# A row scan, its write to DRAM and its read back, moved ahead of some loads; one filler matmul split in two

## The chip, the cores and the metric

The kernel runs on one core of a Trainium2 chip. The time is device time in microseconds, from the first to the last work of the core. The kernel before takes 364.13 us (median of three runs, 364.1 to 365.35). The engines are TensorE (PE; PEld is its loading of stationary operands), VectorE (DVE), ScalarE (ACT), GpSimd (POOL) and SyncE (SP), which here only issues transfers.

## The reference

Two layers follow each other. The first is a chunked scan over 768 steps for 4 batches of 8 heads, with 32 values and 16 states a head:

```python
log_a = np.log(np.clip(a, 1e-06, 1.0))
cum = np.cumsum(la, axis=-1)                      # within a chunk
y_intra = (C B^T * exp(cum_i - cum_j), causal) x
y_inter = (C state) * exp(cum_i)
state = exp(sum(la)) * state + sum_j B_j x_j exp(cum_end - cum_j)
```

(cut and put in short form). Its output, 3072 tokens by 256, goes through the second:

```python
h = x @ w_in                                       # 256 -> 2048
g = np.maximum(h, 0.0) + alpha * np.minimum(h, 0.0)
return (g @ w_out).astype(np.float32)              # 2048 -> 256
```

In place of exponentials of sums the kernel uses running products of `a`: a product from the start of a chunk up to each step is what `exp(cum)` is.

## The kernel before, in words

**Tiling.** The kernel uses chunks of 128 steps (`Q`), six to a batch, and works on pairs of chunks. Pairs 0 and 1 are treated apart, in `first_two`; pair 2 and the later ones go through the generator `pair`, one stage at a time, between the products of the second layer. The second layer takes groups of 512 tokens (two pairs). Group 0 runs in the loop over `f`, 16 blocks of 128 hidden features: `hidden(0, f)` (L1077) multiplies tokens by `w_in` into a PSUM bank of pool `hp`, which has two banks; ScalarE and VectorE make the activation from it (L1080, L1081) and so free the bank; `output(f - 4)` (L1124) multiplies by `w_out`. Later groups run in `quad` and `product`.

**Order.** All five engines keep the order in which the source issues instructions; nothing is rescheduled. An engine that waits holds all that is behind it. All transfers of this part are issued by SP, one after the other. Transfers reuse eight semaphores in turn, so that each also waits for the one eight places earlier.

**Weights.** `w_in` and `w_out` arrive as 16 pieces of 512 KB each (`load_next`, six buffers), and each is converted to f32 by ScalarE, VectorE and GpSimd (`convert_a`, `convert_b`, `convert`; L270 to L327). Pieces 0, 1, 2, 4, 6 belong to `w_in`, 3, 5, 7 to `w_out`.

**Row products.** For half of the batches, `a` lies as 96 rows of 128 steps. `rows_scan(0)` (L462) makes products from each step to the end of its chunk; `rows_products` (L439) makes those from its start, and writes them to a DRAM scratch named `pf` (L442, 48 KB). `load_products` (L167) reads them back, spread over partitions, into the tile `ap` of a pair (128 KB). Pair 2 uses `ap` in `states` (L637, the step of the state) and in `c_decayed` (L677). `load_spread` (L160) reads clamped rows from another scratch, `z`, into the `abc` tiles of a pair (two transfers of 512 KB); the scans L562 make the decays from them. The hp bank that gram L737 of pair 2 writes is the one that L1081 of block 6 reads.

**Where the moved steps stand.** In `first_two`, after pair 0: two pieces of weights, B, C and x of pair 2 for both its chunks (`load_pair(2, False)`), two more pieces; then pair 1; at the end `rows_scan(0)`, `rows_products()`, `load_spread(2, ...)`. The read back into `ap` of pair 2 stands after `first_two`, behind a piece of weights. `convert_next` issues a further piece where the count of loaded pieces allows it.

**Fillers.** `keep_warm(to, n, cols)` (L335) issues n matmuls of ones on `cols` columns into a PSUM place that is not read, so that TensorE is not idle; each shows as two in the profile.

Of the kernel before, what the change touches and what calls it, by code (L numbers as in the profile page):

```python
# [22 lines left out]
def kernel(  # L23
# [25 lines left out]
    nc = tc.nc  # L49
# [7 lines left out]
    Q = 128  # L57
# [4 lines left out]
    RW = batch // 2 * H * CPB  # L62
# [4 lines left out]
    GT = GC * Q  # L67
# [8 lines left out]
    NB = 2  # L76
# [3 lines left out]
    HALF = NP // 2  # L80
# [16 lines left out]
    gp = ctx.enter_context(tc.tile_pool(name="gp", bufs=16))  # L97
# [6 lines left out]
    def bank(i):  # L104


        return ps_q.tile([P, 512], F32, name="bank", tag=f"q{i}")
# [13 lines left out]
    loads = {}  # L121

    def load_rows(i, eng=nc.sync):

        rows = ld.tile([RW, Q], F32, name="rows")
        eng.dma_start(out=rows, in_=a.rearrange("b h (c t) -> (b h c) t", t=Q)[i * RW : (i + 1) * RW])
        loads["r", i] = rows
# [3 lines left out]
    def load_a(t, b, c, eng=nc.sync):  # L131
        first = a[b, 0:1, c * Q : (c + 2) * Q]
        eng.dma_start(out=t, in_=bass.AP(tensor=first.tensor, offset=first.offset,
                                             ap=[[S, H], [0, N], [1, 2 * Q]]))
# [4 lines left out]
    def load_tokens(dst, src, t0):  # L139


        d = dst.rearrange("p j (h w) -> p j h w", h=H)
        for k in range(2):
            for j in range(2):
                t = t0 + k * Q + j * HQ
                nc.sync.dma_start(out=d[HQ * k : HQ * (k + 1), j],
                                  in_=src[:, t : t + HQ, :].rearrange("h p w -> p h w"))

    def load_spread(gp, b, c):

        for w, t in enumerate(loads["p", gp][1] if gp >= HALF else ()):
            rows = scratch["z", b // 2].rearrange("(b h c) t -> b c h t", b=2, h=H)
            for k in range(2):
                nc.sync.dma_start(
                    out=t[HQ * k : HQ * (k + 1), : 4 * SQ].rearrange("p (h t) -> p h t", h=4),
                    in_=rows[b % 2, c + k, 4 * w : 4 * w + 4].unsqueeze(0)
                    .to_broadcast([HQ, 4, SQ]))
        for k, t in enumerate(loads["p", gp][1] if gp < HALF else ()):
            rows = scratch["z", b // 2].rearrange("(b h c) t -> b c h t", b=2, h=H)[b % 2, c + k]
            nc.sync.dma_start(out=t.rearrange("p (h t) -> p h t", h=H),  # L160
                              in_=rows.unsqueeze(0).to_broadcast([P, H, Q]))

    def load_products(gp, ap):
        b, c = divmod(2 * gp, CPB)
        rows = scratch["pf", b // 2].rearrange("(b h c) t -> b h (c t)", b=2, h=H)
        rows = rows[b % 2, :, c * Q : (c + 2) * Q]
        nc.sync.dma_start(out=ap, in_=rows.unsqueeze(1).to_broadcast([H, N, 2 * Q]))  # L167

    def load_pair(gp, decays=True):


        b, c = divmod(2 * gp, CPB)
        turned = gp > GC
        nat = ldx.tile([P, 3, 2, H * N], F32, name="nat")
        xt = ldx.tile([P, 2, HD], F32, name="xt")

        ap = ldx.tile([P, 2 * Q], F32, name="ap")
        if gp == 0:
            load_a(ap, b, c)
        elif gp > NB:  # L180
            load_products(gp, ap)
        if gp == 0:
            load_rows(0, nc.scalar)
        abc = []
        later = []
        if gp >= HALF:
            load_tokens(nat[:, 0], B[b], c * Q)
        for k in range(2 if gp < HALF else 0):
            ts = slice((c + k) * Q, (c + k + 1) * Q)
            for i, src in enumerate((B,) if turned else (B, C)):  # L190
                eng = nc.scalar if gp == 0 and i else nc.sync
                eng.dma_start(out=nat[:, i, k].rearrange("p (h n) -> p h n", h=H),
                              in_=src[b, :, ts, :].rearrange("h p n -> p h n"))

            def load_x(k=k, ts=ts):
                nc.sync.dma_start(out=xt[:, k].rearrange("p (h d) -> p h d", h=H),
                                  in_=x[b, :, ts, :].rearrange("h p d -> p h d"))

            if gp < NB:
                later.append(load_x)  # L200
            else:
                load_x()
        for load_x in later:
            load_x()
        if gp == 0:
            nc.scalar.dma_start(out=al_n, in_=moe_alpha.rearrange("(k p) -> k p", p=P))
            loads["a", 1] = prep.tile([P, 2 * Q], F32, name="a1")
            load_a(loads["a", 1], b, c + 2)
        for i, src in enumerate((B, C) if turned else ()):


            for e in range(2):
                first = src[b, e : e + 1, c * Q : (c + 2) * Q, :]
                nc.sync.dma_start(out=nat[:, 1 + e, i],
                                  in_=bass.AP(tensor=first.tensor, offset=first.offset,
                                              ap=[[2 * S * N, P // 32], [8 * N, 32], [1, 8 * N]]))
        for k in range(2 if gp >= NB else 0):
            abc.append(lda.tile([P, H * Q], F32, name="abc"))
        loads["p", gp] = nat, abc, xt, ap
        if gp >= HALF:  # L220
            load_tokens(xt, x[b], c * Q)
        if decays:
            load_spread(gp, b, c)

    def load_second():

        rows = scratch["short", 0].rearrange("(b h c) t -> b h (c t)", b=2, h=H)
        nc.sync.dma_start(out=loads["p", 1][3], in_=rows[0, :, 2 * Q : 4 * Q].unsqueeze(1)
                          .to_broadcast([H, N, 2 * Q]))
# [102 lines left out]
    def keep_warm(to, n, cols=2 * Q):  # L332

        for i in range(n):
            nc.tensor.matmul(to[:, :cols], warm.to_broadcast([P, P]), warm.to_broadcast([P, cols]),  # L335
                             start=True, stop=True, skip_group_check=True)
# [29 lines left out]
    zeros = const.tile([P, Q], F32, name="zeros")  # L366
# [38 lines left out]
    held = {}  # L405
# [28 lines left out]
        eng.tensor_scalar(out=out, in0=in_, scalar1=1e-6, scalar2=1.0, op0=ALU.max, op1=ALU.min)  # L434

    def rows_products():
        d0 = held.pop(0)
        rpf = prep.tile([RW, Q], F32, name="rpf")
        nc.vector.tensor_tensor_scan(out=rpf, data0=d0[:, :Q], data1=zeros[:RW], initial=1.0,  # L439
                                     op0=ALU.mult, op1=ALU.add)  # L440
        scratch["pf", 0] = dr.tile([RW, Q], F32, name="pf0")
        nc.sync.dma_start(out=scratch["pf", 0], in_=rpf)  # L442
# [98 lines left out]
    def spare():  # L541

        return ps_h.tile([P, GT], F32, name="hp", tag="hp")
# [272 lines left out]
    def first_two():  # L816
# [90 lines left out]
        def mask(i, cs):  # L907
            n = cs.stop - cs.start
            nc.gpsimd.tensor_tensor(
                out=sm[i][:, cs].rearrange("p k (g m) -> p k g m", g=2),  # L910
                in0=new[i][:, cs].unsqueeze(2).to_broadcast([P, n, 2, 2 * D]),
                in1=hmask.rearrange("p (g m) -> p g m", g=2).unsqueeze(1)
                .to_broadcast([P, n, 2, 2 * D]), op=ALU.mult)
# [35 lines left out]
        def ss():  # L949
            return ps_s.tile([P, 512], F32, name="ss")  # L950
# [8 lines left out]
        def one_at_a_time(i, cs):  # L959
            for c in cs:  # L960
                mask(i, slice(c, c + 1))
# [16 lines left out]
        for r in range(4):  # L978
            scan(0, r, sp[r])
        rows_turn("short", prq)  # L980
        tp, hp = spare(), spare()
        bc0 = turned(nat0, (tp, hp))
        cz0 = spread_c(bc0)
        al_p = ss()
        nc.tensor.transpose(al_p[:, :NF], al_n, ident[:NF, :NF])
        nc.scalar.copy(out=alpha, in_=al_p[:, :NF])
        bn0 = pair_loads(0)
        slopes(alpha)
        keep_warm(hp, 1, GT)
        gram_of(bc0, cz0, sp)  # L990
        dps = dps_in([hp, tp])
        added(dps, bn0, xt0)
# [1 line left out]
                                     data1=starts_a, initial=0.0, op0=ALU.mult, op1=ALU.add)  # L994
# [6 lines left out]
            times(0, r, sp[r])  # L1001
        z1 = first_a(loads["a", 1], nc.vector, lent[1][:, 2:])
        load_next(2)
        load_pair(2, False)
        load_next(2)
        convert_a(*pieces[0], by=nc.vector)
        convert_b(*pieces[0], ways=2)
        y = places([ss(), ss()], [hp, tp])
# [28 lines left out]
        added(dps, bn1, xt1)  # L1037
        states(1, dps, pf1, range(3))
        one_at_a_time(1, range(3))
        keep_warm(second, 1)  # L1040

        def among(i, k):
# [16 lines left out]
        convert_next(first=False)  # L1059
        mask(1, slice(3, 4))  # L1060
        held["pr"] = rows_scan(0)
        rows_products()
        load_spread(2, *divmod(4, CPB))
        prelu_of[2]()
        state[0] = new[1][:, 3]
# [334 lines left out]
    def load_next(n=1):  # L1400
        for p in pieces[loaded[0] : loaded[0] + n]:
            load_weights(*p)
        loaded[0] += n
# [13 lines left out]
    load_next(2)  # L1417
    FIRST = 4
    first_two()
    convert_a(*pieces[3])  # L1420
    convert_b(*pieces[3])
    hidden_two(0, 0, 2 * Q, spare())()
    convert_next(first=False)
    load_products(NB, loads["p", NB][3])
    rest = hidden_two(0, 2, 2 * Q, bank(3))
    rows_turn(0, held["pr"])
    convert_a(*pieces[4])
# [135 lines left out]
```

## Time and profile before

| | us |
|---|---|
| median of 3 runs | 364.13 |
| profiled execution | 364.29 |
| its span | 362.6 |
| TensorE busy | 354.0 |
| VectorE busy | 238.1 |
| GpSimd busy | 203.1 |
| ScalarE busy | 172.1 |

Mean granted clock of TensorE: 0.985. The DMA engines are busy for most of the first 58 us, and lightly after. In the profile "x ← y" at the end of a line names what an engine waited for before it; a time in the first column counts from the start of the span.

### The profile page before, as it was taken

How to read it: one execution, taken by the hardware profiler on the slowest of the kernel's cores; microseconds unless marked ns; L12 is line 12 of the kernel's file. 1: busy time of each engine (PE TensorE's matmuls, PEld its weight loads, DVE VectorE, ACT ScalarE, POOL GpSimd, SP SyncE). 2: the span in 40 equal slices, each digit the busy share in tenths (PEclk: the TensorE clock that was granted, in tenths of full speed). 3: DMA queues.
4: the chain of work that ended last, by engine and by line, in shares of the span. 5: the costliest groups of instructions: out<-in, count | busy, mean ns of one | idle time of the engine just before them, and what ended most of it. 6: DMA issues, size and time to landing. Idle time of an engine off the chain costs nothing.

```text
span 362.6 us, 7773 instructions
## 1 busy us (share of the span) xinstructions
PE 354.0 (98%) x2983; PEld 286.6 (79%) x2983; DVE 238.1 (66%) x483; ACT 172.1 (47%) x391; POOL 203.1 (56%) x227
## 2 busy tenths in 40 slices
PE   7999699999999999999999999999999999999996
PEld 3676366667888888888888888888888888888885
DVE  6787575989846856766656766657866634743363
ACT  3379417634445535635535535535535534453431
POOL 6577347669965947554546545537545546334511
PEclk9999969999999999999999999999999999999999
DMA  7999798504525420510640540530301001001102
GB/s 145 192 206 329 229 233 220 136 2 75 170 63 134 88 54 26 102 50 6 116 86 12 109 86 8 112 87 18 57 2 30 1 2 29 2 1 29 33 0 58
DMA packets 105581, 30.24 MB, mean 83 GB/s; under 512 B 79896, under 2 KB 101448, under 8 KB 105544
## 3 DMA queue, kind: packets, MB, share of 16 engines
q1 hardware_dynamic: 103048, 29.43, 35.5%
q10 hardware_dynamic: 2496, 0.32, 0.6%
q8 instruction: 23, 0.38, 0.4%
q14 instruction: 14, 0.11, 0.1%
HBM read 26.32 MB, written 3.42 MB: 82 GB/s over the span
## 4 chain that ended last, share of the span: by engine, by line
PE 90%; DMA 5%; DVE 3%; ACT 1%; SPq 0%; issue 0%; DVEq 0%
PE bank L1198 33%; PE hp L1223 28%; PE bank L1124 7%; PE ss L1223 6%; PE hp L1077 4%; DMA pf<-rpf 2%; PE ss L782 1%; DMA ap<-pf 1%; PE ss L726 1%; DMA nat<-in_B_dram 1%; PE bank L1191 1%; PE ss L800 1%; PE ss L774 1%; PE hp L737 1%; PE ss L737 1%; DVE dec L562 1%
## 5 line engine op out<-in xcount | busy, mean ns | idle before, releaser
L1280 POOL TENSOR_TENSOR gt<-gt 128x512 f32<-128x512 f32 x58 | 74.1, 1278 | 21.1 <-DVE gt L1208 16.3
L1198 PE MATMUL bank<-gt,w_out 128*128 128x256 f32 x320 | 83.5, 381 | 0.0
L1198 PEld LDWEIGHTS bank<-gt,w_out 128*128 128x128 f32 x320 | 60.1, 190 | 9.2 <-issue 1.0
L1208 DVE SCALAR_TENSOR_TENSOR gt<-hp,s_mul,gt 128x256 f32<-128x256 f32 x96 | 42.0, 479 | 29.1 <-ACT gt L1206 26.8
L1270 POOL TENSOR_TENSOR gt<-gt 128x512 f32<-128x512 f32 x20 | 25.4, 1269 | 62.6 <-DVE gt L1208 49.8
L1206 ACT ACTIVATE gt<-hp,s_alpha 128x256 f32<-128x256 f32 x96 | 40.3, 471 | 34.6 <-PE hp L1223 31.5
L1198 PE MATMUL bank<-gt,ws 128*128 128x256 f32 x224 | 55.9, 379 | 0.0
L1198 PEld LDWEIGHTS bank<-gt,ws 128*128 128x128 f32 x224 | 42.3, 190 | 5.6
L1223 PE MATMUL hp<-xs,w_in 128*128 128x256 f32 x160 | 41.9, 384 | 0.0
L1223 PE MATMUL hp<-xs,ws 128*128 128x256 f32 x160 | 41.2, 380 | 0.0
L1249 DVE TENSOR_TENSOR hp<-hp,u 128x512 f32<-128x512 f32 x20 | 14.0, 700 | 35.2 <-ACT u L1247 35.2
L1223 PEld LDWEIGHTS hp<-xs,ws 128*128 128x128 f32 x160 | 30.3, 190 | 4.3 <-POOL xs L1165 0.2
L1223 PEld LDWEIGHTS hp<-xs,w_in 128*128 128x128 f32 x160 | 29.7, 190 | 4.5
L1124 PE MATMUL bank<-w_out,gt 128*128 128x256 f32 x128 | 32.8, 400 | 0.0
L1124 PEld LDWEIGHTS bank<-w_out,gt 128*128 128x128 f32 x128 | 24.8, 199 | 7.1 <-issue 3.9
L640 POOL TENSOR_TENSOR sm<-state,bmask 128x256 f32<-128x256 f32 (+1 forms) x10 | 6.2, 618 | 33.4 <-DVE state L637 33.4
L1223 PE MATMUL ss<-xT,w_in 128*128 128x256 f32 x96 | 24.6, 379 | 0.0
L1077 PE MATMUL hp<-xT,w_in 128*128 128x512 f32 x48 | 23.3, 609 | 0.0
L556 DVE TENSOR_TENSOR_SCAN dec<-abc,bank 128x192 f32<-128x192 f32 x48 | 22.7, 523 | 0.0
L1238 ACT COPY m<-hp 128x512 f32<-128x512 f32 x8 | 4.7, 586 | 35.7 <-PE hp L1223 35.7
L1247 ACT COPY u<-hp 128x512 f32<-128x512 f32 x20 | 11.7, 585 | 19.4 <-PE hp L1223 19.4
L1208 DVE SCALAR_TENSOR_TENSOR gt<-c,s_mul,gt 128x256 f32<-128x256 f32 x40 | 20.6, 556 | 0.0
(230 smaller groups left out, 613.0 us busy)
## 6 DMA issues: line engine op xcount, KB each, us to landing
abc<-z SPq DMA_DIRECT2D x24, 192.0 KB
raw<-in_moe_w_in_dram SPq DMA_DIRECT2D x8, 512.0 KB
raw<-in_moe_w_out_dram SPq DMA_DIRECT2D x8, 512.0 KB
abc<-z SPq DMA_DIRECT2D x8, 512.0 KB
out_dram<-o_sb SPq DMA_DIRECT2D x32, 64.0 KB
nat<-in_B_dram SPq DMA_DIRECT2D x26, 64.0 KB
xt<-in_x_dram SPq DMA_DIRECT2D x12, 128.0 KB
xt<-in_x_dram SPq DMA_DIRECT2D x24, 64.0 KB
```

The source lines that it names most:

```text
L556: nc.vector.tensor_tensor_scan(out=dv[:, o : o + SQ], data0=abc[k][:, s : s + SQ], data1=ident_p[0][:, :SQ], initial=0.0, op0=ALU.mult, op ...
L737: nc.tensor.matmul(gram[r][:, k].rearrange("p h t -> p (h t)"), bh[rs, k], cz[rs, :, k], start=True, stop=True, tile_position=(32 * r, 0), ...
L1077: nc.tensor.matmul(hp, w_in[:, k, f * P : (f + 1) * P], xts[g][:, k], start=(k == 0), stop=(k == KC - 1))
L1124: nc.tensor.matmul(pos[0][t // 2][:, t % 2], gt[:, t * Q : (t + 1) * Q], w_out[:, f], start=(f == 0 and t % 2 == 0), stop=(f == NF - 1), s ...
L1198: nc.tensor.matmul(ms[g][i][:, h], w, blocks[g, z][n][:, p], start=(q == 0 and h == 0), stop=(q == NQ - 1), skip_group_check=True)
L1206: nc.scalar.mul(o[:, p], h[:, p], s_alpha[:, fs[p]])
L1208: nc.vector.scalar_tensor_tensor(out=o[:, p], in0=h[:, p], scalar=s_mul[:, fs[p]], in1=o[:, p], op0=ALU.mult, op1=ALU.max)
L1223: nc.tensor.matmul(to[:, p], w(2 * z + p), b, start=start and p == 0, stop=True, skip_group_check=True)
L1247: nc.scalar.copy(out=u2, in_=A)
L1249: nc.vector.tensor_tensor(out=Y, in0=Y, in1=u2, op=ALU.add)
L1270: nc.gpsimd.tensor_tensor(out=tc_, in0=g22, in1=g12, op=ALU.subtract)
L1280: eng.tensor_tensor(out=o, in0=x0, in1=x1, op=ALU.subtract)
```

## The change

Four edits, all in the first 40 us of the program:

- `load_pair` can be asked for the first chunk of a pair only; it then hands back a function that loads the second.
- `rows_products()` moves from the end of `first_two` to a place behind the first states of pair 1, ahead of pair 1's products with gram (L880). It no longer takes the row tile out of `held`, since `rows_scan(0)` now runs after it.
- Behind it stand, in this order: B, C and x of pair 2's second chunk; three pieces of weights (4, 5, 6); the read of the products into pair 2's `ap`; a piece of weights (7). Of these pieces two stood further ahead, two were issued by `convert_next`; the order of the pieces is the same. The read was issued after `first_two`.
- Of the fillers in pair 0, one of 512 columns ahead of the gram becomes one of 256 columns behind the transpose of alpha, in that transpose's bank, and one of 384 in the old place.

```diff
-    def load_pair(gp, decays=True):
+    def load_pair(gp, decays=True, parted=False):
...
-        for k in range(2 if gp < HALF else 0):
+        def load_natural(k):
             ts = slice((c + k) * Q, (c + k + 1) * Q)
...
+        for k in range((1 if parted else 2) if gp < HALF else 0):
+            load_natural(k)
...
+        return lambda: load_natural(1)
...
     def rows_products():
-        d0 = held.pop(0)
         rpf = prep.tile([RW, Q], F32, name="rpf")
-        nc.vector.tensor_tensor_scan(out=rpf, data0=d0[:, :Q], data1=zeros[:RW], initial=1.0,
+        nc.vector.tensor_tensor_scan(out=rpf, data0=held[0][:, :Q], data1=zeros[:RW], initial=1.0,
                                      op0=ALU.mult, op1=ALU.add)
...
         nc.tensor.transpose(al_p[:, :NF], al_n, ident[:NF, :NF])
+        keep_warm(al_p[:, 2 * Q :], 1)
         nc.scalar.copy(out=alpha, in_=al_p[:, :NF])
         bn0 = pair_loads(0)
         slopes(alpha)
-        keep_warm(hp, 1, GT)
+        keep_warm(hp, 1, 3 * Q)
         gram_of(bc0, cz0, sp)
...
         load_next(2)
-        load_pair(2, False)
-        load_next(2)
+        load_rest = load_pair(2, False, True)
...
         one_at_a_time(1, range(3))
+        rows_products()
+        load_rest()
+        load_next(3)
+        load_products(NB, loads["p", NB][3])
+        load_next()
         keep_warm(second, 1)
...
         held["pr"] = rows_scan(0)
-        rows_products()
         load_spread(2, *divmod(4, CPB))
...
     hidden_two(0, 0, 2 * Q, spare())()
     convert_next(first=False)
-    load_products(NB, loads["p", NB][3])
     rest = hidden_two(0, 2, 2 * Q, bank(3))
```

## The prediction

> **What bounds the kernel now.** I read the page first: its span, the granted clock in 40 slices, and the chain that ended last.
>
> ```profile
> span 362.6 us, 7773 instructions
> ...
> PEclk9999969999999999999999999999999999999999
> ...
> PE 90%; DMA 5%; DVE 3%; ACT 1%; SPq 0%; issue 0%; DVEq 0%
> ```
>
> TensorE sets the time (it is also busy 98% of the span), so a gain must be TensorE time. Only one slice has a low granted clock (the sixth, 45 to 54 us), and 5% of the chain is DMA. The chain in order of time shows where:
>
> ```profile
> 27.13 8.51 DMA pf<-rpf
> ...
> 35.66 4.54 DMA ap<-pf
> ...
> 40.28 0.28 DVE state L637
> 40.56 2.33 DVE dec L562 x4
> ...
> 46.73 3.71 PE bank L1124 x8
> 50.44 2.39 PE hp L1077 x4
> 52.83 1.73 PE bank L1124 x8
> ```
>
> The row products are written to DRAM (8.51 us to land), read back (4.54 us), and VectorE goes on only then; later eight L1124 matmuls take 3.71 us, where the next eight take 1.73. The waits of TensorE in the first 100 us, then VectorE in order of time:
>
> ```profile
> PE hp L737 <- DVE gt L1081: 3.1, 1, 3.1
> ```
>
> ```profile
> 40.28 0.28 DVE L637 SCALAR_TENSOR_TENSOR state<-gt,ap,ss 128x64 f32<-128x64 f32 x1 [4.91 <-DMA ap<-pf]
> 40.48 2.41 DVE L562 TENSOR_TENSOR_SCAN dec<-abc,bank 128x256 f32<-128x256 f32 x4
> ...
> 43.93 0.74 DVE L1081 SCALAR_TENSOR_TENSOR gt<-hp,s_mul,gt 128x512 f32<-128x512 f32 x1
> ```
>
> VectorE stands 4.91 us for `ap`; the L1081 queued behind frees an hp bank late, and TensorE's L737 waits 3.08 us for it (41.65 to 44.73). Busy times by stretch give the aftermath:
>
> ```profile
> 41.40:44.80 3.40, 0.32 (x10) 0.07 (x4) 3.29 (x7) 1.44 (x3) 1.64 (x3) 1.00 0.79 181
> 44.80:48.30 3.50, 3.50 (x14) 2.43 (x15) 3.40 (x7) 0.00 (x0) 1.85 (x3) 0.50 0.82 104
> 48.30:51.70 3.40, 3.40 (x8) 2.16 (x7) 2.81 (x5) 0.00 (x0) 1.62 (x2) 0.51 0.91 252
> 51.70:55.10 3.40, 3.40 (x13) 2.28 (x12) 1.51 (x3) 2.23 (x5) 1.53 (x2) 1.00 1.09 340
> ```
>
> TensorE worked 0.32 of 3.4 us, then had half its clock for 6.8 us. So one late read costs 3.1 us of stall and about 3.4 us of slow clock.
>
> [...]
>
> **The change part by part.** Instruction order is that of the built program.
>
> *Row scan moved.* It now stands on VectorE after three L903 (end 20.27) and ahead of four L880, where VectorE was idle 0.67 us for the gram (20.27 to 20.94). [...] From its old place 1.43 us vanishes; TensorE does not wait there.
>
> *Write moved.* [...] Queued behind: B, C, x of the second half and all later weights. Each goes out about 0.5 us later. The write is behind B, C and one x load; the second half's B, issued where it now stands (21.40), landed at 24.1 by the trace's landing marks (the last of 16 engines). I take 24.
>
> *Read moved.* Now behind pieces 4, 5, 6: SP gets there at about 26.3 (27.13 for the old write, plus 0.5, less two weight issues). The write has been down for 2 us, so pieces 7, 8 and both abc loads behind it don't stall. The data of piece 6 landed at 32.9; the 128 KB (8 descriptors of 1 KB per engine, 46 ns each by the trace's packets, 0.4 us) land at about 33.4 instead of 40.2. L637 is reached at 35.37: `ap` is no longer late.
>
> *What is late next.* The scans L562 behind L637 need the first abc load. It landed at 37.11, unseen behind `ap`. Now it has 0.4 us of `ap` ahead of it and 0.1 of the old write less: 37.5. VectorE waits 1.9 us instead of 4.91, and L562 starts 2.98 us earlier. I take 37.5; bounds 37.1 (nothing added) and 39 (issue on SP pushed out by 1 to 1.5 us).
>
> *Weights.* Piece 4 landed at 29.01 and was used at 29.03, piece 5 31.64 and 31.72. Each lands 0.2 to 0.5 later. Converted, they were ready at 33.23 and 36.14 for matmuls at 35.69 and 37.40: 1.2 us of cover, cost nothing. Pieces 10 and on are further from use.
>
> *Fillers.* Before: one of 512 columns from 7.27 to 9.34 at half clock; the gram started at 9.27, though its input was ready at 8.29. After: 256 columns right after the transpose (about 6.9 to 7.5, in a 0.30 us gap), then 384 columns at half clock (1.6 us), end 9.1: gain 0.2 us. [...]
>
> *The sum* (time from the start of the first scan as before: TensorE resumed at 44.73, 4.25 after 40.48).
> - L737 resumes at 37.5 + 4.25 = 41.75: −2.98.
> - From 44.73 to L792 took 11.55 (2.00 + 3.71 + 2.39 + 1.73 + 1.72). At full clock 1.0 + 1.73 + 1.72 + 1.73 + 1.72 = 7.90: −3.65.
> - VectorE now follows closely. L1081 of the next block frees hp at 37.5 + 7.17 = 44.67, TensorE is there at 44.48: +0.2. Piece 7 is ready on GpSimd 9.65 after the scans' start (50.13 − 40.48), at 47.15; TensorE is there at 46.4: +0.75.
> - The L748 products end at 50.2, before L792 at 50.7: nothing. Later landings (pair 3's abc at 52.5 for scans now at 59.4) are early enough.
>
> Sum −5.7. The profiled execution took 364.29 (span 362.6), the median is 364.13: the same within 0.05%. 364.3 − 5.7 gives 358.6; I forecast 358.7.
>
> **Rivals.**
> - *abc does not bind.* For: it is issued early and the backlog may be shorter. Against: its data follow the same five weights. [...]
> [...]
> [...]
> - *Slower.* The read waits on SP for the write's landing, and pieces 7, 8 and abc are behind it. [...] For: the write took 8.51 before. Against: that was backlog of five weights; now there is 2.5 us of it, giving 24. [...]
>
> **How the numbers follow.** Forecast 0.55; abc not binding 0.12; clock or abc late 0.20; no change 0.07; slower 0.06. Half a per cent, 1.8 us, is about what a measurement can tell from no change. The first three are all under 362.3: faster 0.87. Same 0.07, slower 0.06. The range runs from the second case less some early gain, 356.9, to the late cases with some of both (clock 1.7 and abc 0.5 on top), 361.5; it leaves out no change and slower.
>
> **What would show it.** L637 without a DMA wait, and L562 instead waiting about 2 us for abc; L737's wait of 3.1 us under 0.8; granted clock 1.00 from 41 to 55, and eight L1124 matmuls in 1.73; a wait of 0.7 us on piece 7's w_out. Wrong would be: a wait on SP at the read; abc after 39; a half-clock window after 41; TensorE idle before 41.

## The result, and the profile after

The changed kernel takes 360.07 us (median of 6 runs, 358.8 to 361.69) against 364.51 for the kernel before on the same chip (6 runs, 362.79 to 366.55): a ratio of 0.9876, 95% interval 0.9833 to 0.9918. The forecast was 358.7. The profiled execution took 359.63 us against 364.29 before.

The page of the changed kernel: span, granted clock in 40 slices, and the chain that ended last, by engine.

```profile
span 357.9 us, 7776 instructions
...
PEclk9999999999999999999999999999999999999999
...
PE 91%; DMA 4%; DVE 2%; ACT 1%; SPq 1%; POOL 0%; issue 0%; DVEq 0%
```

The slice with the low clock is gone, yet the chain still holds 4% of DMA. The chain in order of time says which transfer this is now (start, length, what):

```profile
29.05 8.99 DMA abc<-z
...
47.77 1.99 PE bank L1131 x8
```

The write and the read of the row products have left the chain; the load of `abc`, which lay unseen behind them, stands in their place. The eight products with `w_out` that had taken 3.71 us take 1.99. VectorE in order of time (start, length, what; in brackets the idle time before it and what ended it):

```profile
36.40 0.27 DVE L640 SCALAR_TENSOR_TENSOR state<-gt,ap,ss 128x64 f32<-128x64 f32 x1
38.07 2.42 DVE L565 TENSOR_TENSOR_SCAN dec<-abc,bank 128x256 f32<-128x256 f32 x4 [1.40 <-DMA abc<-z]
```

L640 (L637 before) no longer waits for `ap`. The scans behind it wait 1.40 us for `abc` and start at 38.07 instead of 40.48. The two waits of TensorE that matter here (in total, times, longest):

```profile
PE ss L627 <- POOL bn L531: 0.9, 1, 0.9
...
PE hp L740 <- DVE gt L1088: 0.7, 1, 0.7
```

The wait of 3.1 us has become 0.7, and a wait of 0.9 us that was not there before, on `bn`, lies ahead of it. TensorE's work by stretch (columns: the stretch; its us and PE busy; PEld, DVE, ACT and POOL busy; granted clock; DMA share; GB/s):

```profile
41.40:44.80 3.40, 2.73 (x23) 1.96 (x18) 3.40 (x7) 1.46 (x3) 2.51 (x3) 1.00 0.79 174
44.80:48.30 3.50, 3.05 (x9) 1.33 (x8) 3.29 (x7) 0.93 (x2) 1.27 (x1) 1.00 0.82 104
48.30:51.70 3.40, 3.40 (x34) 2.00 (x40) 3.29 (x6) 2.66 (x6) 1.90 (x2) 1.00 0.96 264
```

Before, TensorE was busy for 0.32 us of the first stretch and then ran at half clock through the other two (0.50 and 0.51). Now it is busy for 2.73 us of it and keeps its full clock.

SP's queue (start, time that the issue took, what) shows where the moved transfers stand; `raw` is piece 4 of the weights:

```profile
21.57 0.52 SPq L445 DMA_DIRECT2D pf<-rpf  x1
...
24.89 0.64 SPq L258 DMA_DIRECT2D raw<-in_moe_w_in_dram  x1
...
26.65 0.60 SPq L167 DMA_DIRECT2D ap<-pf  x1
```

Piece 4 in the kernel before:

```profile
23.43 0.58 SPq L254 DMA_DIRECT2D raw<-in_moe_w_in_dram  x1
```

SP stood still before neither of the two moved transfers: the write followed the issue of the x load by 0.1 us (21.47 to 21.57), and the read went out at 26.65, when the write had been down for two microseconds (24.57 by the landing marks).

### The profile page after: what moved, and what is told of

It reads as the page before. It is cut to its first block, busy times and chain, and to the rows that moved or that the text cites. A ratio compares the mean times of both kernels' runs of the same rounds, so it can differ in the third digit from the quotient of the medians.

```text
span 357.9 us, 7776 instructions
## 1 busy us (share of the span) xinstructions
PE 350.4 (98%) x2985; PEld 284.3 (79%) x2985; DVE 237.7 (66%) x483; ACT 172.2 (48%) x391; POOL 203.1 (57%) x227
## 4 chain that ended last, share of the span: by engine, by line
PE 91%; DMA 4%; DVE 2%; ACT 1%; SPq 1%; POOL 0%; issue 0%; DVEq 0%
PE bank L1205 33%; PE hp L1230 28%; PE bank L1131 6%; PE ss L1230 6%; PE hp L1084 3%; DMA abc<-z 3%; PE hp L1099 2%; PE ss L785 1%; DVE dec L565 1%; PE ss L729 1%; DMA nat<-in_B_dram 1%; PE bank L1198 1%; PE ss L803 1%; PE ss L777 1%; PE ss L740 1%; PE bank L339 1%
## 5 line engine op out<-in xcount | busy, mean ns | idle before, releaser
L1131 PE MATMUL bank<-w_out,gt 128*128 128x256 f32 x128 | 31.2, 386 | 0.6 <-POOL w_out L331 0.6
L1131 PEld LDWEIGHTS bank<-w_out,gt 128*128 128x128 f32 x128 | 23.5, 190 | 7.7 <-issue 2.6
```

The lines of the kernel that those rows point to most:

```text
L1131: nc.tensor.matmul(pos[0][t // 2][:, t % 2], gt[:, t * Q : (t + 1) * Q], w_out[:, f], start=(f == 0 and t % 2 == 0), stop=(f == NF - 1), s ...
```

## The experiments

My theory: the gain is the end of the wait for `ap` plus the half clock that followed that wait; it needs the read early on SP with pieces of weights between write and read; what bounds the rest is `abc`. The rivals: the two short fillers, or the early write alone, make the gain; or the stall alone matters and the clock does not.

The clock can be counted in every run, not only in profiled ones: each run has a mean granted clock. In the profile of the kernel before TensorE has half its clock from 7.29 to 10.70 us and from 44.83 to 51.66, for 3.41 and 6.83 us. I count 3.41 us at half clock as one half-clock window; it lowers the mean by 1.71 / 363 = 0.0047. The kernel before ran 51 times beside the first experiments. By the number of half-clock windows in a run (rounded), the medians are: none 361.25 (1 run), one 362.54 (11), two 364.02 (28), three 365.10 (11). So each window goes with about 1.3 us, on the average over the places where such windows lie; the mean number is 1.96. (The profiled execution of before, with 0.985, comes to three, as those two stretches do.)

### The fillers alone, and the change without them

The first run is the kernel before with the two short fillers:

```diff
         nc.tensor.transpose(al_p[:, :NF], al_n, ident[:NF, :NF])
+        keep_warm(al_p[:, 2 * Q :], 1)
...
-        keep_warm(hp, 1, GT)
+        keep_warm(hp, 1, 3 * Q)
```

> The kernel before with the two short fillers alone. Theory (the late read of the row products sets the time, and what TensorE gains ahead of it is waited off at L737): no change in time, ratio 0.998 to 1.002; the start up to the first xT copies may come up to 1.4 us earlier, and L737's wait grows by as much. Rival (the gain is the early full clock): 1.0 to 1.4 us less than before.

Measured: 364.31 against 364.0, ratio 1.0 (0.9974 to 1.0026). The time is as expected, but the step named for it is not what the profile shows: the wait at L737 had not grown, it was nearly gone.

```profile
PE hp L737 <- DVE gt L1082: 0.3, 1, 0.3
```

That execution took 360.65 us, the shortest of the 14. `ap` came at 38.91 instead of 40.28, TensorE was later by itself (it had waited 1.0 us, to 22.13, and its two L1093 from 23.59 took 0.83 us, where the same two take 0.64 with the long filler of the next run). Its mean clock of 0.995 comes to one half-clock window, and eight L1125 from 48.80 took 1.99 us, as in the changed kernel. So the old order can come near the changed kernel's time in an execution in which the stall is small; where a typical run of the fillers loses what they gain is not shown.

The second is the changed kernel with the one long filler back (the same lines the other way round).

> The changed kernel with the one long filler of 512 columns put back. Theory (the abc load bounds): the same 4 to 4.7 us gain as the changed kernel, since TensorE has 0.94 and 0.67 us of waits ahead of the abc scans' end to lose first; it starts 0 to 1.4 us later, and the waits shrink by as much. Rival (the early full clock is part of the gain): only 3 to 3.5 us less than before.

Measured: 359.25 against 364.0, ratio 0.9882 (0.9845 to 0.9918), not to be told from the changed kernel's 0.9876. The fillers have no measurable part in the gain, together with the other edits or without them.

### The write early, the read where it was

The kernel before with `rows_products()` moved ahead of the products with gram, and nothing else:

```diff
         one_at_a_time(1, range(3))
+        rows_products()
...
         held["pr"] = rows_scan(0)
-        rows_products()
```

> The kernel before with the scan and the write of the row products in their new place, the loads and the read back left as they were. Theory: the read stands in the queue behind the abc loads and a piece of weights, so it still lands at about 40; no gain, ratio 0.997 to 1.003, VectorE still waits over 4 us for ap. Rival (the late write is the cause): at least 2 us less than before.

Measured: 364.43, ratio 1.0015 (0.9992 to 1.0037): no gain. VectorE in order of time:

```profile
40.55 0.28 DVE L636 SCALAR_TENSOR_TENSOR state<-gt,ap,ss 128x64 f32<-128x64 f32 x1 [5.32 <-DMA ap<-pf]
```

On SP the call's new place brought the write forward by only 0.8 us (26.35 instead of 27.13), since the loads ahead of it were the same. The read was issued at 34.20 instead of 35.66, behind an issue of weights that took 3.29 us, and took 6.25 us in the chain instead of 4.54. So an earlier write alone gains nothing: the read stands in SP's queue where it stood.

### Write and read early, with the pieces of weights left ahead of them

As the last one, with the read directly behind the write; all loads of pair 2 and pieces 4 to 7 stay ahead of both:

```diff
         one_at_a_time(1, range(3))
+        rows_products()
+        load_products(NB, loads["p", NB][3])
...
-    load_products(NB, loads["p", NB][3])
```

> The kernel before with scan, write and read all early, but with pair 2's loads and the pieces of weights left ahead of them, so that the write is behind four pieces in the queue. Theory: the write lands at about 34, SP stands at the read until then, and piece 8 and abc are issued only after it; abc lands at 39.5 to 41, so 0 to 1 us less than before. Rival (where the loads stand does not matter): the gain of the changed kernel, 4 to 4.7 us.

Measured: 364.81, ratio 1.0021 (0.9993 to 1.0049). SP's queue, and then VectorE:

```profile
26.65 0.41 SPq L441 DMA_DIRECT2D pf<-rpf  x1
33.85 0.60 SPq L167 DMA_DIRECT2D ap<-pf  x1
```

```profile
36.74 0.28 DVE L636 SCALAR_TENSOR_TENSOR state<-gt,ap,ss 128x64 f32<-128x64 f32 x1 [1.82 <-DMA ap<-pf]
42.02 2.42 DVE L561 TENSOR_TENSOR_SCAN dec<-abc,bank 128x256 f32<-128x256 f32 x4 [5.00 <-DMA abc<-z]
```

This is the prediction's "slower" rival made real: SP stands from 27.06 to 33.85 for the write to land behind the weights, and `abc`, queued behind the read, goes out at 35.13 instead of 29.05. What `ap` gains, `abc` loses (it came about 1 us later than I had expected), and TensorE's wait is 4.9 us. In the changed kernel the write goes out 5 us sooner with few bytes ahead, and three pieces of weights are issued while it lands: that is what makes the move pay. It is not the split of pair 2's loads: with the write behind the loads of both chunks, and the pieces still behind it, the time is the same (360.06, below).

### The stall left in, the clock kept up

The kernel before, with three fillers of 512 columns in TensorE's queue ahead of the gram of pair 2, where it waits:

```diff
             gram = {r: ss_tile() if r < small else spare() for r in range(4)}
+            if gp == NB:
+                for i in range(3):
+                    keep_warm(gram[0], 1, GT)
```

> The kernel before with three more filler matmuls of 512 columns (3.2 us) ahead of pair 2's gram, in a bank that the gram then overwrites: TensorE waits for hp as before, but is not idle meanwhile. Theory: the half clock after the wait goes, 3.65 us, less 0.1 to 0.2 of fillers in excess and 0.75 for the w_out of piece 7: 2.5 to 2.9 us less than before, granted clock 1.00 from 41 to 55 us. Rival (the clock costs nothing, since VectorE sets that stretch): no change.

Measured: 362.48 against 364.0, ratio 0.9955 (0.9936 to 0.9974): 1.5 us gained, where I expected 2.5 to 2.9. VectorE still waited 5.57 us for `ap`. By stretch:

```profile
41.40:44.80 3.40, 2.66 (x11) 0.87 (x9) 3.30 (x7) 1.27 (x3) 1.76 (x3) 1.00 0.96 227
44.80:48.30 3.50, 2.53 (x17) 2.01 (x18) 3.50 (x7) 0.00 (x0) 2.49 (x3) 1.00 0.89 113
```

The clock holds, though VectorE's stall is there as before. The mean number of half-clock windows fell from 1.96 to 0.86 over 22 runs; at 1.3 us each that is 1.4 us, about the measured gain. So the half clock is a real part of what the late read cost, apart from the stall; but it is worth less than the profiled execution suggests: that one had two such windows behind the stall, and the fillers took away 1.1 a run in the mean.

### What bounds the changed kernel now

Three places for the load of `abc`. First one piece of weights sooner: the changed kernel with

```diff
         load_products(NB, loads["p", NB][3])
         load_next()
+        load_spread(2, *divmod(4, CPB))
...
         held["pr"] = rows_scan(0)
-        load_spread(2, *divmod(4, CPB))
```

> The changed kernel with the two abc loads of pair 2 issued ahead of piece 8 of the weights. Theory (abc bounds what is left): abc lands some 1.7 us earlier, the scans follow L640 at once at about 36.7 in place of 38.07, the waits of 0.67 at L740, 0.2 at hp and most of 0.44 at w_out go: 0.8 to 1.3 us less than the changed kernel, 5 to 6 less than before. Rival (TensorE is late by itself, through bn): the same as the changed kernel.

Measured: 358.6 against 364.15, ratio 0.9855 (0.9814 to 0.9895). VectorE:

```profile
36.66 2.42 DVE L565 TENSOR_TENSOR_SCAN dec<-abc,bank 128x256 f32<-128x256 f32 x4 [1.55 <-DMA abc<-z]
```

The scans start 1.41 us earlier than in the first profile of the changed kernel, and TensorE's wait at L740 is 0.4. Next, the write put behind the loads of the second chunk, since that trace of the changed kernel shows the DMA engines nearly idle just behind the write. Its stretch of one microsecond, and the same stretch in a second profile of the same kernel (columns as above; the last but one is the DMA share):

```profile
23.00:24.00 1.00, 1.00 (x7) 0.87 (x6) 0.47 (x4) 0.97 (x4) 0.85 (x1) 1.00 0.24 49
```

```profile
23.00:24.00 1.00, 1.00 (x17) 0.93 (x17) 0.84 (x4) 0.21 (x1) 0.05 (x1) 1.00 0.91 120
```

Before, the share from 23 to 24 was 1.32. The dip belongs to the first of the two executions, and not to the place of the write.

```diff
+        load_rest()
         rows_products()
-        load_rest()
```

> The changed kernel with the write issued behind the second half of pair 2's loads in place of ahead of them. Theory (the write ahead of these loads leaves the DMA engines idle for about 0.8 us, 23 to 24 us): piece 4 lands 0.8 to 1.4 us earlier, the wait of 0.94 for bn goes, abc lands 0.5 us earlier: 0.4 to 0.7 us less than the changed kernel, the wait at L740 growing to about 1. Rival (the idle stretch is there without the write): no change from the changed kernel.

> The changed kernel with both edits: abc ahead of piece 8, and the write behind the second half of the loads. Theory: the waits for bn (0.94), at L740 (0.67), at hp (0.2) and most of that for w_out (0.44) go together: 1.7 to 2.2 us less than the changed kernel, 6 to 7 less than before. Rival (one of the two covers the other): no more than the better of them alone.

Measured: the write behind alone 360.06, ratio 0.9898 (0.9851 to 0.9945); with `abc` sooner as well 358.4, 0.9844 (0.9805 to 0.9883). On SP the write now goes out behind the second chunk's loads, and pieces 4 to 6 still follow it (from 24.49) ahead of the read (27.27):

```profile
23.70 0.75 SPq L445 DMA_DIRECT2D pf<-rpf  x1
```

The share from 23 to 24 was filled in this kernel (1.23), but the gain of 0.4 to 0.7 us that I had expected did not follow, and the two together gained 5.8 us over before, where I had expected 6 to 7. The profiled execution of the first was disturbed by a wait of 1.5 us in TensorE at 21 to 22.5 (last section), and half clock followed it: the granted clock was 0.54 from 23 to 24 us and 0.50 from 24 to 26, and eight L1099 from 29.15 took 2.16 us, where eight from 14.49 took 1.73. A stretch of it:

```profile
23.40:26.80 3.40, 3.40 (x17) 2.84 (x16) 0.26 (x2) 1.90 (x7) 1.57 (x2) 0.50 0.97 178
```

So that profile gives no verdict on what the place of the write is worth.

The last set ran on one chip: the changed kernel again, both variants again, and `abc` one piece later, which is in the changed kernel

```diff
         held["pr"] = rows_scan(0)
-        load_spread(2, *divmod(4, CPB))
...
     hidden_two(0, 0, 2 * Q, spare())()
     convert_next(first=False)
+    load_spread(2, *divmod(4, CPB))
```

> The changed kernel again, beside the next three on one chip. Theory and rival alike: 0.984 to 0.991 of the kernel before, as measured.

> The changed kernel with pair 2's abc loads one piece of weights sooner, again. Theory (abc bounds what is left): 0.8 to 1.5 us less than the changed kernel beside it. Rival (TensorE is late by itself): within 0.4 us of it.

> The changed kernel with abc sooner and the write behind the second half of the loads, again. Theory: at least as fast as abc sooner alone, 1 to 2 us less than the changed kernel beside it. Rival (the write's place matters nothing once abc is sooner): within 0.4 us of abc sooner alone.

> The changed kernel with pair 2's abc loads one piece of weights later. Theory: abc lands about 1.7 us later, the scans start at about 39.8, L740 waits 2.4 us in place of 0.67, and TensorE falls to half clock after it in some runs (1.4 us a window): 1.7 to 3.2 us more than the changed kernel beside it. Rival: within 0.4 us of it.

| kernel | median, us | ratio to before (364.67) | interval | half-clock windows, mean |
|---|---|---|---|---|
| `abc` sooner | 357.83 | 0.9830 | 0.9794 to 0.9865 | 0.33 |
| `abc` sooner, write behind | 358.06 | 0.9822 | 0.9790 to 0.9855 | 0.20 |
| as changed | 359.96 | 0.9876 | 0.9833 to 0.9918 | 0.33 |
| `abc` later | 361.36 | 0.9922 | 0.9895 to 0.9949 | 1.11 |

With `abc` one piece later, VectorE and TensorE's wait read:

```profile
39.02 2.42 DVE L565 TENSOR_TENSOR_SCAN dec<-abc,bank 128x256 f32<-128x256 f32 x4 [3.20 <-DMA abc<-z]
```

```profile
PE hp L740 <- DVE gt L1087: 2.5, 1, 2.5
```

The order of the times is the order of the loads. With `abc` later the stall is back and half-clock windows are more frequent: of its 1.4 us over the changed kernel (I had expected 1.7 to 3.2), 0.78 windows more at 1.3 us would be 1.0. Where these windows lie is not seen; its profiled execution has none. With `abc` sooner, the write's place again makes no difference that can be told (0.2 us). The version with `abc` sooner has the lowest median in this set. How much it gains over the changed kernel stays open: 2.1 us by the medians here, where I had expected 0.8 to 1.5; in the first sets it gained 5.6 us over before and the changed kernel 4.4, on different chips. The intervals overlap, and the two profiled executions of this set differ by only 0.4 us (357.99 and 358.39), and so do the starts of their scans (36.45 and 36.85). In that second profile of the changed kernel the scans waited 1.37 us for `abc`, but TensorE did not wait at L740 at all, having lost 1.5 us to waits at 17 to 22.5 us. So `abc` holds VectorE in both profiles, and TensorE in one of them.

## Why the prediction was right, and where it missed

The time of 360.07 lies in the range and on the foretold side of before, 1.4 us above the forecast. By the prediction's own steps, each in the two profiled executions:

| step | forecast | measured |
|---|---|---|
| `ap` no longer late at L637/L640 | yes | yes |
| scans start | 37.5 (−2.98) | 38.07 (−2.41) |
| from the scans' start to TensorE at L737/L740 | 4.25 | 4.25 (42.32) |
| from there to L792/L795 | 8.85 | 9.09 (51.41) |
| of this: waits for the hp bank and for piece 7's `w_out` | 0.2, 0.75 | 0.2, 0.44 |
| of this: the matmuls | 7.90 | 8.5 |
| whole execution | −5.7 | −4.66 |

Two sums of the prediction do not come out, and neither changes it: its terms put L792 at 50.6, not 50.7; and 358.7 + 1.7 + 0.5 is 360.9, where its range ends at 361.5. Two terms of that range no run shows: the 1.7 us of the clock, where a half-clock window went with about 1.3 us over the runs of before, and the early gain at its lower end, where the fillers alone gave 364.31 against 364.0.

**The order of events was right.** `ap` drops out, `abc` takes its place as the wait that ends last, TensorE resumes at the same distance behind the scans, and the clock stays up. The early write and read made SP wait for nothing. The rival in which `abc` does not bind falls in this profile (1.40 us of waiting in VectorE, 0.67 in TensorE); in the second profile it falls for VectorE alone. The clock did not fall in either profile of the changed kernel (mean 1.000 in both). Of its 12 runs five have one half-clock window. Where in the run it lies is not seen there; in the profiles of the two variants with the write behind, the clock is low from 23 us on (0.50 from 24 to 26 in the one, 0.58 and 0.56 from 24.40 to 27.80 in the two of the other).

**The landing was 0.57 us late in the first profile, through SP's issues.** I had each load go out about 0.5 us later, and had moved the landing of `abc` by 0.4. Piece 4 went out at 24.89 instead of 23.43 and landed at 30.47 instead of 29.01, both 1.46 later; `abc` went out at 29.05 instead of 28.11, 0.94 later, and took 8.99 us to land, where it had taken 9.00. Between the write and piece 4, SP spent 1.26 and 0.77 us on issuing B and C, before 0.58 on each. Piece 4's lateness held up VectorE by 2.21 us (its conversion started at 30.49) and then `bn` and TensorE, 0.94 us at L627; the wait for `abc` covers that, since TensorE then still waits at L740. This is not a fixed cost of the change: in the profiles with the long filler and with `abc` sooner, which issue these transfers in the same order, B and C took 0.43 and 0.58 or 0.59 us, and with the long filler `abc` went out at 28.24 and took 9.06 us, to 37.30. In the second profile of the changed kernel the scans, which wait for `abc` there too, start at 36.85, and TensorE has no wait for `bn`. The forecast of 37.5 lies between the two executions; why SP's issues take longer in one profile than in others stays open.

**The term of the clock was mis-sized.** The sum took 3.65 us off the matmuls behind the stall (11.55 to 7.90). In the profiled pair they took 8.5, so about 3.0 went. The profile of before was also not a typical run: TensorE's stall (41.65 to 44.73) lay almost wholly in the last 3.41 us at full clock (41.42 to 44.83, TensorE busy for 0.33 us of them), and two half-clock windows followed. Over many runs on one chip the kernel before has 2.21 windows and the changed one 0.33 (14 and 6 runs), a difference of 1.88, at 1.3 us each 2.4 us. The gain there is 364.67 − 359.96 = 4.7, so about 2.3 are left for the stall, where the forecast had 2.98 less 0.95 of new waits, 2.0. This division is a fit on medians and prices all windows alike, though one that lies ahead of a wait can cost little, as in the profile of the fillers alone; of its two parts only the clock's was measured by itself (1.5 us for 1.1 windows).

**The row scan and the fillers were rightly costed at nothing.** The sum has no term for either. The scan took 0.68 us, where the equal scan L462 took 0.42 in before, and was over at 19.41, when L883 could start at 19.48 without a wait. The gram of pair 0 started at 8.37 instead of 9.27, more than the forecast's 0.2 us: the granted clock was 1.00 from 7.3 to 10.7, where it was 0.50 in before. The fillers alone brought nothing to the total; that the wait behind them swallows their gain, as I had expected of that run, is argued and not shown.

## What to carry to other kernels

Here a late transfer cost TensorE the stall and, in many runs, a slow clock after it, and the clock's part was measured apart by fillers in the place of the wait. Price the clock from many runs and not from one profile. When a transfer is moved ahead, ask which load stands next behind it in the same queue: here moving a write and its read back paid with loads issued between them and did not without, and the next load then bound what was left. Take the landing of a transfer from more than one profile too: the scans that wait for `abc` started 1.2 us apart in two executions of one kernel (38.07 and 36.85).

## What I had not expected of the hardware

- The number of half-clock windows of one and the same kernel differs from run to run, 0 to 3 in the kernel before, and its time rises with it (361.25 to 365.10 by the medians of the groups), though runs with two windows alone still spread from 362.19 to 365.91. In the profile of before the clock changes at 7.29, 10.70, 44.83 and 51.66 us, which lie 3.41, 34.13 and 6.83 us apart: one, ten and two times 3.41. The trace's first record of the clock stands at 3.87 us, again 3.41 us ahead of the first change; in the changed kernel it stands at 4.76, and the mean clock is 1.000. With `abc` later, TensorE was busy for 2.80 us from 38.00 to 41.40 and for 1.53 us from 41.40 to 44.80, with its wait of 2.5 us in between, and the granted clock stayed at 1.00 up to 58.50. In before TensorE was busy for 0.33 us of the 3.41 from 41.42 to 44.83, and half clock followed.
- The busy time of such a stretch alone does not decide. In before, 3.41 us with 2.38 busy (3.87 to 7.29) were followed by half clock, and with `abc` later 3.40 us with 1.53 (41.40 to 44.80) were not. So no threshold can be read from these traces, and TensorE need not have been idle for the clock to be halved.
- In five profiled executions (the fillers alone, the changed kernel with the long filler, the write behind, and twice the write behind with `abc` sooner) TensorE waited 1.0 to 1.5 us at about 21 to 22.5 us, with an instruction of VectorE named as releaser that had been done, or none. In four of them half clock followed from about 23 or 24 us, by the mean clocks (0.995, 0.989, 0.995, 0.995) for one window or two; with the long filler none did (0.999). The wait is absent from the profile of the kernel before and from the first of the changed kernel, and up to 0.8 us in others. Its cause stays open; it hides in the wait for `abc` where that wait is long.
